# Attention and two expert layers on one core: four query chunks among the key chunks, another count of zeros, one reduction for the sums of squares

## The chip, the cores and the metric

The kernel runs on one core of one Trainium2 chip. The metric is the device time of one execution in microseconds (us); less is better. The engines are named as the profile names them: PE is TensorE's matmul, PEld its weight load, DVE is VectorE, ACT is ScalarE, POOL is GpSimd, and SP is SyncE, which issues every DMA of this kernel from one queue.

## What is computed

A kernel-feature attention feeds two layers one after the other. There are 4 x 576 = 2304 tokens, 8 heads of 64, 128 features, a model width of 512 and an inner width of 2048. All is float32.

```python
def phi(x):                                    # for queries and keys, scaled by D ** -0.25
    proj = np.einsum('bhsd,md->bhsm', x, omega)
    sq = np.sum(x * x, axis=-1, keepdims=True) / 2.0
    h = proj - sq
    h = h - np.max(h, axis=-1, keepdims=True)
    return np.exp(h) / np.sqrt(m)
kv = np.einsum('bhsm,bhsd->bhmd', k_p, v)
z = np.sum(k_p, axis=2)
num = np.einsum('bhsm,bhmd->bhsd', q_p, kv)
den = np.einsum('bhsm,bhm->bhs', q_p, z)[..., None] + 1e-06
x = num / den                                  # then tokens x 512
h = x @ w_in;  x = (h * np.cos(h)) @ w_out     # first layer
h = x @ w2_in; y = (h * np.clip(h + 3, 0, 6) / 6) @ w2_out   # second layer
```

## The kernel before

**Tiles and stages.** The tokens are cut into 18 chunks of 128. For each of 18 key chunks `chunk("k", c, ...)` loads a transposed tile `xT`, a plain tile `nat` and a value tile `v`; POOL squares `nat` and adds halves (L324, L328); DVE sums what is left per head into `sq` (`sums`, L334); PE projects `xT` with `omd` into two PSUM banks (L350); DVE takes the maximum per head (L363) and forms the bias (L370, L374); ACT takes the exponential of the two banks into two tiles `P` (L388, four instructions each); PE multiplies `P` with `v` into the running sums `kv` of a batch (L403). A query chunk goes the same way as far as `P`, is then transposed on PE (L433), copied by ACT into `qt`, multiplied with the finished `kvs` of its batch (L446), normalised on DVE (`rd`, `xn`: L456, L460, L467), transposed back (L481) and copied by ACT into `xx`. A query chunk needs the `kvs` of its batch only, and a batch is 4.5 chunks long.

The first layer's first half (8 of 16 inner tiles) of the first 1024 tokens runs as 16 "pair slots" (L711 into the bank `h`, L737 out to `kv`) between the query chunks. A slot's nonlinearity is two DVE steps (L651, L657), a sine on ACT (L661), a product on DVE (L664), a rounding on ACT and a difference on DVE. Exponentials and sines use different tables on ACT, so the sines of two slots stand behind the exponentials of two query chunks. After the last query chunk come "slots" of up to 512 tokens (L780 in, L802 out). All weights arrive as 64-bit numbers (`ws`, 512 KB a half tile) and are turned into two float32r parts by ACT and by five DVE steps (L559, L563, L569, L575, L261).

**What sets the order.** Nothing is scheduled on the chip. `Plan.order` plays the program through on the host: each task has a key (a due time in us), a modelled duration on its engine, and rings of buffers (`RINGS`); at each moment an engine takes the task with the smallest key that can start. The result is the order of instructions on each engine. A key chunk's key is `T_K * c`, a query chunk's `t_q + T_Q * p + 3 * (c % 2)` with `t_q = T_K * NCH`, so query chunks follow the key chunks. A key chunk's two banks come in turn from the rings `at`, `pt` and `h` of two banks each; a query chunk's from `at` alone.

**Zeros.** Where the plan has PE idle, the last loop puts matmuls of a zero tile (64 columns) on PE, whose results are not used: L872 while a `kv` sum is open, L875 while a pair slot's sum is open, L881 else. Their number is the planned idle time times `FILL_SHARE`, divided by `T_FILL`:

```python
for _ in range(int((now - idle) * FILL_SHARE / T_FILL) if f else 0):
```

One zero is one MATMUL of the program and two rows of the trace, since a float32 matmul runs in two passes.

Of the kernel before, what the change touches and what calls it, by code (L numbers as in the profile page):

```python
# [12 lines left out]
ALU = mybir.AluOpType  # L13
# [22 lines left out]
N_WARM = 5  # L36
N_PAIR = NCH // 2
N_A = 4
# [11 lines left out]
W_GATE = {}  # L50
PER = 2
FILL = 64
T_FILL = 0.115
FILL_SHARE = 0.8
LAT = {"t": 0.27, "a": 0.17, "v": 0.13, "p": 0.15, "d": 2.0}
# [142 lines left out]
def attention_moe_moe2_kernel(  # L198
# [95 lines left out]

    t_q = T_K * NCH

    def chunk(kind, c, k, exp_after, lead):
        u = (kind, c)
# [17 lines left out]

        pr = ("at", "pt", "h")[c % 3] if isk else "at"

        def square(e):
# [9 lines left out]

        def sums(e):  # L330

            sq = tile_of(ap, SQ, "sq", [128, 8])
            for hf in range(2):
                nc.vector.tensor_reduce(  # L334
                    out=sq[:, 4 * hf:4 * hf + 4], in_=buf[A].rearrange("p (h d) -> p h d", h=8)[:, hf:8:2, 0:32], axis=AX.X, op=ALU.add
                )

        add(("sqn",) + u, k - 3.5, {"p": 1.1}, square, use=[A])
        add(("sqh",) + u, k - 2, {"p": 0.7}, halve, [("sqn",) + u], use=[A])
        add(SQ, k - 0.5, {"v": 0.5}, sums, [("sqh",) + u], alloc="sq", use=[A])  # L340

        P0, P1 = ("pj", kind, c, 0), ("pj", kind, c, 1)
        before = [("pj", kind, c - 1, 1)] if c else [] if isk else [("pj", "k", NCH - 1, 1)]
        add(P0, k - 0.2, {"t": 0.01}, lambda e: bank(P0, pr), before, alloc=pr, use=[X])
# [23 lines left out]
        def bias1(e):  # L368
            mx = buf[MX]
            nc.vector.scalar_tensor_tensor(out=mx[:, 8:16], in0=buf[SQ], scalar=-0.5 * SCALE * SCALE, in1=mx[:, 0:8], op0=ALU.mult, op1=ALU.add)  # L370

        def bias2(e):
            mx = buf[MX]
            nc.vector.scalar_tensor_tensor(out=mx[:, 16:24], in0=buf[SQ], scalar=-0.5 * SCALE * SCALE, in1=mx[:, 8:16], op0=ALU.mult, op1=ALU.subtract)  # L374

# [3 lines left out]
        for hf in range(2):  # L379
            E = ("e", kind, c, hf)  # L380

            def exps(e, hf=hf, E=E):
                pj, mx = buf["pj", kind, c, hf], buf[MX]
                p = tile_of(ap, E, "P", [128, 512])
                for h in range(4):
                    o = slice(128 * h, 128 * h + 128)
                    b = 16 + 4 * hf + h
                    nc.scalar.activation(out=p[:, o], in_=pj[:, o], func=ACTF.Exp, bias=mx[:, b:b + 1])  # L388

            add(E, k + 1.5 + 0.1 * hf, {"a": 1.25 + (1.3 if exp_after and hf == 0 and c % PER == 0 else 0.0)}, exps,  # L390
                [("b2",) + u] + exp_after + ([("e", kind, c, 0)] if hf else []), alloc="P", use=[("pj", kind, c, hf), MX])
# [98 lines left out]

    for c in range(NCH):
        chunk("k", c, T_K * c, [], 6)
    n_a = N_A * NG // 2

    def period(g):

        return 1 + g // 2 if PER == 2 else min(3 + g, NCH - 1)

    for c in range(NCH):
        p = c // 2  # L500
        prior = [("sn", g) for g in range(n_a) if period(g) == c // PER - 1]
# [193 lines left out]
    def pair_slot(g):  # L695
# [259 lines left out]
```

## Time and profile before

| | us |
|---|---|
| median of 3 runs | 998.49 |
| lowest and highest | 998.3, 999.55 |
| the profiled execution, its own time | 997.92 |
| its span, first to last instruction | 996.1 |
| PE busy in the span | 985.5 |
| DVE, ACT, POOL busy | 599.0, 441.4, 90.6 |

A row of the timeline gives start and duration in us, the engine, the line, what it writes from what, shapes and count; behind it in brackets the idle time of the engine just before and what ended it. The ends of matmuls are modelled and overlap the next one's start, so a group's length is read from its start to the next one's start. A row of the stretches gives for each engine the busy time, the granted clock of PE as a share of full speed, and the busy share and rate of the DMA engines.

### The profile page before, as it was taken

How to read it: one execution, taken by the hardware profiler on the slowest of the kernel's cores; microseconds unless marked ns; L12 is line 12 of the kernel's file. 1: busy time of each engine (PE TensorE's matmuls, PEld its weight loads, DVE VectorE, ACT ScalarE, POOL GpSimd, SP SyncE). 2: the span in 40 equal slices, each digit the busy share in tenths (PEclk: the TensorE clock that was granted, in tenths of full speed). 3: DMA queues.
4: the chain of work that ended last, by engine and by line, in shares of the span. 5: the costliest groups of instructions: out<-in, count | busy, mean ns of one | idle time of the engine just before them, and what ended most of it. 6: DMA issues, size and time to landing. Idle time of an engine off the chain costs nothing.

```text
span 996.1 us, 16910 instructions
## 1 busy us (share of the span) xinstructions
PE 985.5 (99%) x6830; PEld 860.1 (86%) x6830; DVE 599.0 (60%) x1207; ACT 441.4 (44%) x888; POOL 90.6 (9%) x103
## 2 busy tenths in 40 slices
PE   9999999999999999999999999999999999999998
PEld 8899998989898889888888898888888888888898
DVE  5887788545569998999956599723223222322322
ACT  4775566555654545444332344424223322422332
POOL 5542134100000000010000000000000000000000
PEclk9999999999999999999999999999999999999999
DMA  8974344111012333332311014101000100100010
GB/s 278 331 246 151 107 136 140 33 44 33 2 42 86 110 101 107 106 117 81 118 55 43 1 50 132 64 1 43 1 1 1 42 1 1 43 1 1 1 43 22
DMA packets 32269, 72.59 MB, mean 73 GB/s; under 512 B 3392, under 2 KB 7488, under 8 KB 32192
## 3 DMA queue, kind: packets, MB, share of 16 engines
q1 hardware_dynamic: 32192, 71.52, 22.1%
q8 instruction: 53, 0.87, 0.4%
q14 instruction: 24, 0.20, 0.1%
HBM read 62.07 MB, written 9.44 MB: 72 GB/s over the span
## 4 chain that ended last, share of the span: by engine, by line
PE 97%; ACT 1%; DMA 1%; issue 0%; SPq 0%
PE at L780 18%; PE pt L780 18%; PE kv L802 18%; PE h L802 18%; PE h L711 5%; PE kv L737 5%; PE kv L881 3%; PE kv L872 3%; PE pt L446 2%; PE at L350 2%; PE kv L403 2%; PE kv L875 2%; PE pt L433 1%; PE pt L481 1%; DMA ws<-w 1%; PE pt L350 1%
## 5 line engine op out<-in xcount | busy, mean ns | idle before, releaser
L261 DVE TENSOR_TENSOR gl<-wk,gh 128x512 fp32r<-128x512 f32 (+1 forms) x160 | 104.3, 652 | 127.1 <-ACT gh L254 119.5
L254 ACT ACTIVATE gh<-wk 128x512 fp32r<-128x512 f32 (+1 forms) x160 | 94.4, 590 | 157.2 <-PE h L802 122.7
L780 PE MATMUL at<-mxh,wl 128*128 128x512 f32 (+1 forms) x288 | 105.3, 366 | 0.0
L780 PE MATMUL at<-mxh,wh 128*128 128x512 f32 (+1 forms) x288 | 105.3, 366 | 0.0
L802 PE MATMUL kv<-gh,wl 128*128 128x512 f32 (+1 forms) x288 | 105.3, 366 | 0.0
L802 PE MATMUL kv<-gh,wh 128*128 128x512 f32 (+1 forms) x288 | 105.3, 366 | 0.0
L780 PE MATMUL pt<-mxh,wl 128*128 128x512 f32 (+1 forms) x288 | 105.3, 366 | 0.0
L802 PE MATMUL h<-gh,wl 128*128 128x512 f32 (+1 forms) x288 | 105.3, 365 | 0.0
L780 PE MATMUL pt<-mxl,wh 128*128 128x512 f32 (+1 forms) x288 | 105.2, 365 | 0.0
L780 PE MATMUL at<-mxl,wh 128*128 128x512 f32 (+1 forms) x288 | 105.2, 365 | 0.0
L802 PE MATMUL kv<-gl,wh 128*128 128x512 f32 (+1 forms) x288 | 105.2, 365 | 0.0
L780 PE MATMUL pt<-mxh,wh 128*128 128x512 f32 (+1 forms) x288 | 105.2, 365 | 0.0
L802 PE MATMUL h<-gl,wh 128*128 128x512 f32 (+1 forms) x288 | 105.2, 365 | 0.0
L802 PE MATMUL h<-gh,wh 128*128 128x512 f32 (+1 forms) x288 | 105.2, 365 | 0.0
L661 ACT ACTIVATE wk<-wk,halfpi 128x512 f32<-128x512 f32 (+1 forms) x80 | 54.4, 681 | 91.5 <-DVE wk L657 91.3
L256 POOL TENSOR_SCALAR mxh<-xx 128x512 fp32r<-128x512 f32 (+1 forms) x25 | 20.3, 813 | 666.2 <-DVE mxl L261 258.0
L678 DVE SCALAR_TENSOR_TENSOR wk<-wk,at 128x512 f32<-128x512 f32 (+1 forms) x40 | 25.4, 635 | 70.3 <-ACT wk L672 70.2
L678 DVE SCALAR_TENSOR_TENSOR wk<-wk,pt 128x512 f32<-128x512 f32 (+1 forms) x40 | 25.4, 636 | 67.2 <-ACT wk L672 66.9
L780 PEld LDWEIGHTS pt<-mxh,wl 128*128 128x128 f32 x288 | 54.4, 189 | 8.9
L802 PEld LDWEIGHTS h<-gh,wh 128*128 128x128 f32 x288 | 54.4, 189 | 8.9
L780 PEld LDWEIGHTS pt<-mxh,wh 128*128 128x128 f32 x288 | 54.3, 189 | 8.9
L780 PEld LDWEIGHTS at<-mxl,wh 128*128 128x128 f32 x288 | 54.3, 189 | 8.9
(97 smaller groups left out, 2069.0 us busy)
## 6 DMA issues: line engine op xcount, KB each, us to landing
ws<-w SPq DMA_DIRECT2D x64, 512.0 KB, 3.7
v<-vn SPq DMA_DIRECT2D x18, 260.0 KB, 4.5
nat<-kn SPq DMA_DIRECT2D x18, 256.0 KB, 5.2
xT<-qT SPq DMA_DIRECT2D x18, 256.0 KB, 2.8
nat<-qn SPq DMA_DIRECT2D x18, 256.0 KB, 3.7
xT<-kT SPq DMA_DIRECT2D x17, 256.0 KB, 5.2
yy<-yp SPq DMA_DIRECT2D x16, 256.0 KB, 2.2
yp<-yy SPq DMA_DIRECT2D x16, 256.0 KB, 4.0
```

The costliest lines, as they stand in the source:

```text
L254: nc.scalar.activation(out=o, in_=i, func=ACTF.Copy)
L256: nc.gpsimd.tensor_scalar(out=o, in0=i, scalar1=1.0, scalar2=0.0, op0=ALU.mult, op1=ALU.add)
L261: (nc.gpsimd if e == "p" else nc.vector).tensor_tensor(out=o, in0=a, in1=b, op=ALU.subtract)
L350: nc.tensor.matmul(out=buf["pj", kind, c, o][:, 128 * i:128 * i + 128], lhsT=buf[X][64 * o:64 * o + 64, 128 * i:128 * i + 128], rhs=omd[64 ...
L661: nc.scalar.activation(out=r, in_=r, func=ACTF.Sin, scale=-TURN, bias=halfpi)
L678: nc.vector.scalar_tensor_tensor(out=w, in0=w, scalar=6.0, in1=hb(), op0=ALU.min, op1=ALU.mult)
L711: nc.tensor.matmul(out=o, lhsT=w[:, 128 * kc:128 * kc + 128], rhs=v, start=(kc == 0 and j == 0), stop=(kc == KC - 1 and j == 2), skip_grou ...
L737: nc.tensor.matmul(out=y, lhsT=w[:, o], rhs=v, start=(first and fi == 0 and j == 0 and ec % 2 == 0), stop=(last and fi == 1 and j == 2 and ...
L780: nc.tensor.matmul(out=buf["h", g][:, :n], lhsT=w[:, 128 * kc:128 * kc + 128], rhs=x, start=(kc == 0 and j == 0), stop=(kc == KC - 1 and j ...
L802: nc.tensor.matmul(out=buf["y", bi, ec][:, :n], lhsT=w[:, o], rhs=x, start=(first and j == 0), stop=(last and j == 2),)
L872: return lambda: nc.tensor.matmul(out=buf["kv", b, hf][:, 0:FILL], lhsT=zero[:, 0:128], rhs=zero[:, 0:FILL], start=False, stop=False, skip ...
L881: return lambda: nc.tensor.matmul(out=buf["fill", ring][:, 0:FILL], lhsT=zero[:, 0:128], rhs=zero[:, 0:FILL], start=True, stop=True)
```

## The change

There are three edits. (1) The first four query chunks (`N_EARLY`) stand in the planner's sequence at places 6, 8, 10 and 12 (`K_EARLY`), among the key chunks. `before` links of the projections follow that sequence. From place 6 on, the banks alternate between `at` and `h`, since `pt` is now used by the transposes; the first six key chunks still use three rings. `t_q` grows by four `T_K`, the query chunks after them and the pair slots get new due times (the first two slots' sines now stand behind the exponentials of query chunks 4 and 5, not 2 and 3). (2) The number of zeros is computed from 0.24 us for each, after 0.5 us of the gap are left out, rounded. (3) `sums` reduces all eight heads in one instruction; the bias steps read the sums through a reordered view.

```diff
-N_PAIR = NCH // 2
+N_EARLY = 4
+K_EARLY = 6
-PER = 2
-T_FILL = 0.115
-FILL_SHARE = 0.8
+T_FILL = 0.24
+FILL_SKIP = 0.5
...
-    t_q = T_K * NCH
+    t_q = T_K * (NCH + N_EARLY)
...
-        pr = ("at", "pt", "h")[c % 3] if isk else "at"
...
-            for hf in range(2):
-                nc.vector.tensor_reduce(
-                    out=sq[:, 4 * hf:4 * hf + 4], in_=buf[A].rearrange("p (h d) -> p h d", h=8)[:, hf:8:2, 0:32], axis=AX.X, op=ALU.add
-                )
+            nc.vector.tensor_reduce(out=sq, in_=buf[A].rearrange("p (h d) -> p h d", h=8)[:, :, 0:32], axis=AX.X, op=ALU.add)
...
-        add(SQ, k - 0.5, {"v": 0.5}, sums, [("sqh",) + u], alloc="sq", use=[A])
+        add(SQ, k - 0.5, {"v": 0.38}, sums, [("sqh",) + u], alloc="sq", use=[A])
...
-        before = [("pj", kind, c - 1, 1)] if c else [] if isk else [("pj", "k", NCH - 1, 1)]
+        before = [("pj",) + prev + (1,)] if prev else []
...
-    for c in range(NCH):
-        chunk("k", c, T_K * c, [], 6)
...
-        return 1 + g // 2 if PER == 2 else min(3 + g, NCH - 1)
-
-    for c in range(NCH):
-        p = c // 2
-        prior = [("sn", g) for g in range(n_a) if period(g) == c // PER - 1]
-        chunk("q", c, t_q + T_Q * p + 3 * (c % 2), prior, 10)
+        return N_EARLY // 2 + 1 + g // 2
+
+    order = [("k", c) for c in range(NCH)]
+    for c in range(N_EARLY):
+        order.insert(K_EARLY + 2 * c, ("q", c))
+    prev = None
+    for i, (kind, c) in enumerate(order):
+        pr = ("at", "pt", "h")[i % 3] if i < K_EARLY else ("at", "h")[i % 2]
+        chunk(kind, c, T_K * i, [], 6 if kind == "k" else 10, pr, prev)
+        prev = (kind, c)
+    for c in range(N_EARLY, NCH):
+        prior = [("sn", g) for g in range(n_a) if period(g) == c // 2]
+        chunk("q", c, t_q + T_Q * ((c - N_EARLY) // 2) + 3 * (c % 2), prior, 10, "at", prev)
+        prev = ("q", c)
...
-                slots.append((bi, 2 * fp, t_q + T_Q * (1 + s // 2) + 8 * (s % 2)))
+                slots.append((bi, 2 * fp, t_q + T_Q * (s / 2) + 4))
...
-        sn_after = [("e", "q", c, hf) for c in range(NCH) for hf in range(2) if c // PER == period(g)]
+        sn_after = [("e", "q", c, hf) for c in range(NCH) for hf in range(2) if c // 2 == period(g) - 1]
...
-                    for _ in range(int((now - idle) * FILL_SHARE / T_FILL) if f else 0):
+                    for _ in range(int((now - idle - FILL_SKIP) / T_FILL + 0.5) if f else 0):
```

The program of before has 294 zeros, that of after 66. Up to the first pair slot's matmul it has 208 and 44, behind that 86 and 22. Of real work PE has, up to that matmul, 168 projection matmuls, 320 value products, 28 transposes and 32 query products before, and 184, 304, 48 and 64 after; the work of all stages together is the same.

On PE, in the middle of the key chunks, before (L350 is a projection, L403 a product with values, L872 zeros; the numbers in names are buffers):

```order
L350 MATMUL at<-omd,xT 128x128 x8
L403 MATMUL kv_774<-v,P 64x65 x8
L872 MATMUL kv_774<-zero 128x64 x4
L350 MATMUL pt<-omd,xT 128x128 x8
L403 MATMUL kv_833<-v,P 64x65 x8
L403 MATMUL kv_774<-v,P 64x65 x8
L872 MATMUL kv_774<-zero 128x64 x4
L350 MATMUL h<-omd,xT 128x128 x8
L403 MATMUL kv_833<-v,P 64x65 x8
L872 MATMUL kv_774<-zero 128x64 x10
L403 MATMUL kv_774<-v,P 64x65 x8
L872 MATMUL kv_774<-zero 128x64 x8
```

and after, a little earlier in the key chunks (L351, L404 and L879 are the same three; L434, L447 and L482 are a query chunk's transposes, its product and its transpose back):

```order
L434 MATMUL pt<-ident,P 128x128 x4
L447 MATMUL pt<-kvs,qt 64x65 x8
L404 MATMUL kv_460<-v,P 64x65 x8
L447 MATMUL pt<-kvs,qt 64x65 x8
L351 MATMUL h<-omd,xT 128x128 x8
L404 MATMUL kv_493<-v,P 64x65 x8
L482 MATMUL pt<-ident,xn 128x128 x4
L434 MATMUL pt<-ident,P 128x128 x4
L879 MATMUL kv_460<-zero 128x64 x4
L351 MATMUL at<-omd,xT 128x128 x8
```

A query chunk's four kinds of PE work now stand between two key chunks, with few zeros or none, and the projections go to two rings in turn.

On PE, from the last key chunk's products to the first pair slot, before:

```order
L403 MATMUL kv_1169<-v,P 64x65 x8
L881 MATMUL kv_1381<-zero 128x64 x10
L433 MATMUL pt<-ident,P 128x128 x4
L881 MATMUL kv_1381<-zero 128x64 x6
L350 MATMUL at<-omd,xT 128x128 x8
L433 MATMUL pt<-ident,P 128x128 x4
L446 MATMUL pt<-kvs,qt 64x65 x8
L881 MATMUL kv_1381<-zero 128x64 x8
L446 MATMUL pt<-kvs,qt 64x65 x8
L881 MATMUL kv_1381<-zero 128x64 x17
L481 MATMUL pt<-ident,xn 128x128 x4
```

and after (L718 is L711 of before):

```order
L351 MATMUL at<-omd,xT 128x128 x8
L404 MATMUL kv_1439<-v,P 64x65 x8
L879 MATMUL kv_1382<-zero 128x64 x5
L718 MATMUL h<-mxh,wh_77 128x256
L718 MATMUL h<-mxh,wl_78 128x256
L718 MATMUL h<-mxl,wh_77 128x256
L718 MATMUL h<-mxh,wh_77 128x256
L718 MATMUL h<-mxh,wl_78 128x256
L718 MATMUL h<-mxl,wh_77 128x256
L404 MATMUL kv_1382<-v,P 64x65 x8
```

The stretch of query chunks with nothing but zeros between their steps is gone; the first pair slot starts before the last key chunk's products.

On DVE, in the key chunks, before (L363 the maxima, L334 the sums):

```order
L363 TENSOR_REDUCE mx<-pt 128x4
L575 SCALAR_TENSOR_TENSOR wt<-ws,wt 128x512
L370 SCALAR_TENSOR_TENSOR mx<-sq,mx 128x8
L334 TENSOR_REDUCE sq<-nat 128x4 x2
L374 SCALAR_TENSOR_TENSOR mx<-sq,mx 128x8
```

and after (L364 the maxima, L330 the sums, L457, L461 and L468 a query chunk's normalising):

```order
L364 TENSOR_REDUCE mx<-h 128x4
L582 SCALAR_TENSOR_TENSOR wt<-ws,wt 128x512
L371 SCALAR_TENSOR_TENSOR mx<-sq,mx 128x8
L330 TENSOR_REDUCE sq<-nat 128x8
L375 SCALAR_TENSOR_TENSOR mx<-sq,mx 128x8
L364 TENSOR_REDUCE mx<-at 128x4
L261 TENSOR_TENSOR wl_80<-wt,wh_79 128x512
L457 TENSOR_SCALAR rd<-pt 128x4
```

One reduction stands where there were two, and a query chunk's steps stand among those of the key chunks. Ahead of the first pair slot's L651 (L658 after), DVE has 44 maxima, 44 sums, 42 bias steps, 53 steps on `wt`, 13 on `wl` and 12 normalising steps before, and 46, 24, 46, 49, 10 and 24 after. Ahead of the first sine, ACT has 176 exponentials, 6 `qt`, 2 `xx`, 13 `wh` and 16 `wt` before, and 192, 11, 5, 12 and 15 after. SP issues, ahead of the last value tile, 9 halves of weights and 6 query tiles before, 12 and 13 after.

## Rows read from the trace of the kernel before

**Rows 1.** The page's first part: busy time of each engine, its share of the span, instructions.

```profile
PE 985.5 (99%) x6830; PEld 860.1 (86%) x6830; DVE 599.0 (60%) x1207; ACT 441.4 (44%) x888; POOL 90.6 (9%) x103
```

**Rows 2.** Who waited for whom, PE, 0 to 300 us: us in total, times, longest.

```profile
PE pt L446 <- ACT qt L254: 3.3, 3, 1.1
```

**Rows 3.** Groups of instructions by line, PE, the zeros: count, busy us, mean ns, idle before.

```profile
L872 PE MATMUL kv<-zero 128*128 128x64 f32 x216 | 28.6, 280 | 0.0
L881 PE MATMUL kv<-zero 128*128 128x64 f32 x228 | 27.8, 275 | 0.5 <-ACT kvs L254 0.5
L875 PE MATMUL kv<-zero 128*128 128x64 f32 x144 | 17.2, 275 | 0.0
```

**Rows 4.** Timeline of PE: three runs of zeros and what follows each.

```profile
44.75 2.44 PE L872 MATMUL kv<-zero 128*128 128x64 f32 x20
47.13 1.16 PE L350 MATMUL at<-omd,xT 64*128 64x128 f32 x16
...
93.56 4.01 PE L881 MATMUL kv<-zero 128*128 128x64 f32 x34
97.41 0.61 PE L481 MATMUL pt<-ident,xn 128*128 128x128 f32 x4
...
102.72 3.79 PE L881 MATMUL kv<-zero 128*128 128x64 f32 x32
106.34 0.61 PE L481 MATMUL pt<-ident,xn 128*128 128x128 f32 x4
```

**Rows 5.** Timelines of ACT and DVE: the work that the matmuls behind those zeros need (the exponentials that free the bank `at`, and the normalised tiles).

```profile
44.69 1.14 ACT L388 ACTIVATE P<-at,mx 128x128 f32<-128x128 f32 x4
...
94.75 0.42 DVE L467 TENSOR_TENSOR xn<-pt,rd 128x256 f32<-128x256 f32 x1
...
103.98 0.41 DVE L467 TENSOR_TENSOR xn<-pt,rd 128x256 f32<-128x256 f32 x1
```

**Rows 6.** Timelines of DVE, ACT and PE: the first maximum, the first exponentials, the first matmul of a pair slot, its first DVE step, the first sine, the first matmul of a slot.

```profile
6.50 0.69 DVE L363 TENSOR_REDUCE mx<-at 128x4 f32<-128x512 f32 x1 [3.70 <-PE at L350]
10.33 1.28 ACT L388 ACT_TABLE_LOAD   x1 [10.33 <-DVE mx L374]
110.89 0.37 PE L711 MATMUL h<-mxh,wh 128*128 128x256 f32 x1
115.50 0.69 DVE L651 TENSOR_SCALAR wk<-h 128x512 f32<-128x512 f32 x1 [0.47 <-PE h L711]
121.85 0.72 ACT L661 ACTIVATE wk<-wk,halfpi 128x512 f32<-128x512 f32 x1
290.49 0.40 PE L780 MATMUL at<-mxh,wh 128*128 128x512 f32 x1
```

**Rows 7.** The chain that ended last, 84 to 125 us: start, us that count on the chain, what.

```profile
88.79 1.09 PE at L350 x16
93.02 0.62 PE pt L446 x16
97.57 0.44 PE pt L481 x4
...
113.11 2.35 PE h L711 x18
```

**Rows 8.** Busy time in stretches: PE, PEld, DVE, ACT and POOL (with counts), granted clock, DMA share, GB/s.

```profile
30.00:40.00 10.00, 8.58 (x138) 7.57 (x138) 8.10 (x21) 6.89 (x23) 3.48 (x4) 1.00 0.99 342
0.00:115.50 115.50, 111.88 (x1538) 102.88 (x1539) 87.39 (x213) 69.60 (x213) 50.89 (x59) 1.00 0.70 232
0.00:121.80 121.80, 118.18 (x1611) 108.73 (x1612) 92.30 (x227) 74.19 (x224) 50.89 (x59) 1.00 0.68 223
10.00:84.00 74.00, 72.39 (x1154) 66.32 (x1150) 61.30 (x152) 53.69 (x174) 40.81 (x42) 1.00 0.84 280
84.00:111.00 27.00, 26.51 (x291) 25.26 (x286) 19.58 (x48) 13.67 (x36) 6.21 (x8) 1.00 0.37 119
121.80:290.60 168.80, 165.53 (x1766) 154.86 (x1765) 106.76 (x271) 104.56 (x224) 26.10 (x27) 1.00 0.20 61
300.00:500.00 200.00, 200.00 (x973) 169.42 (x973) 184.83 (x343) 95.71 (x162) 7.86 (x10) 1.00 0.32 103
```

**Rows 9.** Timeline of DVE in the key chunks: two sums, a bias step, a maximum, a step on `wt`.

```profile
62.63 0.46 DVE L334 TENSOR_REDUCE sq<-nat 128x4 f32<-128x128 f32 x2
63.01 0.15 DVE L370 SCALAR_TENSOR_TENSOR mx<-sq,mx 128x8 f32<-128x8 f32 x1
...
64.68 0.68 DVE L363 TENSOR_REDUCE mx<-at 128x4 f32<-128x512 f32 x1
65.28 0.68 DVE L569 SCALAR_TENSOR_TENSOR wt<-ws,wt 128x512 uint32<-128x512 uint32 x1
```

**Rows 10.** Timelines of PE and ACT: the seventh key chunk's projection; the exponentials of the key chunk that was projected into `at` at 47.13, and the next projection into `at`.

```profile
22.97 1.16 PE L350 MATMUL at<-omd,xT 64*128 64x128 f32 x16
...
54.31 1.15 ACT L388 ACTIVATE P<-at,mx 128x128 f32<-128x128 f32 x4 [1.85 <-DVE mx L374]
59.02 0.66 ACT L555 ACTIVATE wt<-ws 128x512 f32<-128x512 f32 x1 [3.56 <-DMA ws<-w]
59.58 1.14 ACT L388 ACTIVATE P<-at,mx 128x128 f32<-128x128 f32 x4
...
60.69 1.24 PE L350 MATMUL at<-omd,xT 64*128 64x128 f32 x16
```

More of the change, by code (lines that the diff above doesn't have):

```diff
@@ L293, in attention_moe_moe2_kernel, with chunk @@
     kv_parts = {(b, hf): [] for b in range(B) for hf in range(2)}
-    t_q = T_K * NCH
-    def chunk(kind, c, k, exp_after, lead):
+    t_q = T_K * (NCH + N_EARLY)
+    def chunk(kind, c, k, exp_after, lead, pr, prev):
         u = (kind, c)
@@ L332, in sums, with sq_of, four @@
             sq = tile_of(ap, SQ, "sq", [128, 8])
-            for hf in range(2):
-                nc.vector.tensor_reduce(
-                    out=sq[:, 4 * hf:4 * hf + 4], in_=buf[A].rearrange("p (h d) -> p h d", h=8)[:, hf:8:2, 0:32], axis=AX.X, op=ALU.add
-                )
+            nc.vector.tensor_reduce(out=sq, in_=buf[A].rearrange("p (h d) -> p h d", h=8)[:, :, 0:32], axis=AX.X, op=ALU.add)
+        def sq_of():
+            return buf[SQ].rearrange("p (i o) -> p o i", o=2)
+        def four(a):
+            return a.rearrange("p (o i) -> p o i", o=2)
         add(("sqn",) + u, k - 3.5, {"p": 1.1}, square, use=[A])
         add(("sqh",) + u, k - 2, {"p": 0.7}, halve, [("sqn",) + u], use=[A])
-        add(SQ, k - 0.5, {"v": 0.5}, sums, [("sqh",) + u], alloc="sq", use=[A])
+        add(SQ, k - 0.5, {"v": 0.38}, sums, [("sqh",) + u], alloc="sq", use=[A])
         P0, P1 = ("pj", kind, c, 0), ("pj", kind, c, 1)
-        before = [("pj", kind, c - 1, 1)] if c else [] if isk else [("pj", "k", NCH - 1, 1)]
+        before = [("pj",) + prev + (1,)] if prev else []
         add(P0, k - 0.2, {"t": 0.01}, lambda e: bank(P0, pr), before, alloc=pr, use=[X])
@@ L369, in bias1 @@
             mx = buf[MX]
-            nc.vector.scalar_tensor_tensor(out=mx[:, 8:16], in0=buf[SQ], scalar=-0.5 * SCALE * SCALE, in1=mx[:, 0:8], op0=ALU.mult, op1=ALU.add)
+            nc.vector.scalar_tensor_tensor(out=four(mx[:, 8:16]), in0=sq_of(), scalar=-0.5 * SCALE * SCALE, in1=four(mx[:, 0:8]), op0=ALU.mult, op1=ALU.add)
         def bias2(e):
             mx = buf[MX]
-            nc.vector.scalar_tensor_tensor(out=mx[:, 16:24], in0=buf[SQ], scalar=-0.5 * SCALE * SCALE, in1=mx[:, 8:16], op0=ALU.mult, op1=ALU.subtract)
+            nc.vector.scalar_tensor_tensor(out=four(mx[:, 16:24]), in0=sq_of(), scalar=-0.5 * SCALE * SCALE, in1=four(mx[:, 8:16]), op0=ALU.mult, op1=ALU.subtract)
         add(("b1",) + u, k + 1.2, {"v": 0.2}, bias1, [("mx", kind, c, 1)], use=[MX, SQ])
@@ L388, in exps @@
                     nc.scalar.activation(out=p[:, o], in_=pj[:, o], func=ACTF.Exp, bias=mx[:, b:b + 1])
-            add(E, k + 1.5 + 0.1 * hf, {"a": 1.25 + (1.3 if exp_after and hf == 0 and c % PER == 0 else 0.0)}, exps,
+            add(E, k + 1.5 + 0.1 * hf, {"a": 1.25 + (1.3 if exp_after and hf == 0 and c % 2 == 0 else 0.0)}, exps,
                 [("b2",) + u] + exp_after + ([("e", kind, c, 0)] if hf else []), alloc="P", use=[("pj", kind, c, hf), MX])
@@ L489, in chunk @@
         add(("xx", c), k + 7.5, {"a": 0.62}, put, use=[("xt", c)])
-    for c in range(NCH):
-        chunk("k", c, T_K * c, [], 6)
     n_a = N_A * NG // 2
     def period(g):
-        return 1 + g // 2 if PER == 2 else min(3 + g, NCH - 1)
-    for c in range(NCH):
-        p = c // 2
-        prior = [("sn", g) for g in range(n_a) if period(g) == c // PER - 1]
-        chunk("q", c, t_q + T_Q * p + 3 * (c % 2), prior, 10)
+        return N_EARLY // 2 + 1 + g // 2
[11 more added lines that the diff above has]
+        prev = ("q", c)
     all_exp = [("e", "q", c, hf) for c in range(NCH) for hf in range(2)]
     all_att = [("xx", c) for c in range(NCH)]
-    t_m = t_q + T_Q * N_PAIR
+    t_m = t_q + T_Q * (NCH - N_EARLY) / 2 + 8
     blocks = [dict(m=1, t0=256 * b, n=256, fs=range(0, NG), mode="pair") for b in range(N_A)]
-    blocks += [dict(m=1, t0=t0, n=n, fs=range(0, NG), mode="part") for t0, n in ((1024, 512), (1536, 512), (2048, 256))]
+    blocks += [dict(m=1, t0=t0, n=n, fs=range(0, NG), mode="part") for t0, n in [(t0, min(512, NT - t0)) for t0 in range(256 * N_A, NT, 512)]]
     n_g1 = len(blocks)
```

## The prediction

> **What bounds the kernel now.** I read the busy times first: PE works for 985.5 of 996.1 us, every other engine at most 60% [rows 1]. Then the waits: PE's longest kind in the first 300 us comes to 3.3 us in total [rows 2]. So the time is PE's list of instructions, and what matters is what is in it. The groups by line show 216 + 228 + 144 = 588 rows of zeros [rows 3], 294 instructions, all before the first slot of 512 columns at 290.49 [rows 6]. Behind that point nothing is changed, and PE is 100% busy at least to 500 us [rows 8]. So I looked at how long a zero takes, and at whether the thing that it waits for is late or early.
>
> A zero's length is read from start to start. The three runs take 2.38, 3.85 and 3.62 us for 10, 17 and 16 zeros, together 9.85 us for 43, or 0.229 us each [rows 4]. (Two rows a zero, so about 0.115 us a row: the planner of before counted one of the two.) And the zeros run past what they wait for. The exponentials that free the bank `at` end at 45.83, the projection into it starts at 47.13. The normalised tiles end at 95.17 and 104.39, their transposes start at 97.41 and 106.34 [rows 4, 5]. That is 1.3, 2.2 and 2.0 us late: 5.5 of 9.85 us, or 56%, was surplus, and the rest covers a real wait.
>
> **The zeros.** 294 become 66: 228 x 0.23 = **52.4 us** of PE's list go, 164 x 0.23 = 37.7 ahead of the first pair slot, 64 x 0.23 = 14.7 behind it. This is the most that the change can give on PE. Not all of it stays: where a zero covered a wait, the wait comes back as idle time.
>
> The page "TensorE: Matmul & The Clock Gate" of the Trainium skill, section "Back-to-back issue gap", gives a warm matmul its columns over 2.4 GHz plus 2.5 ns; for 64 columns that is an estimate of 29 ns a row, and the removed zeros would be worth 13 us. Its section "LDWEIGHTS" gives a load 128 columns over 1.2 GHz, 107 ns by estimate, and with that the removed zeros are worth 49 us. The runs of zeros decide for the second: a row takes 115 ns [rows 4].
>
> **The early query chunks.** They move work ahead of the first pair slot. The instruction counts there change by +16 projections, -16 value products, +20 transposes and +32 query products. By the chain's rows these cost 1.09 / 8, 0.62 / 8 (a value product has the same 65 columns), 0.44 / 4 and 0.62 / 8 us [rows 7]: 2.2 - 1.2 + 2.2 + 2.5 = +5.7 us ahead, and 5.7 less behind. What is bought: between 84 and 111 us PE did nearly nothing but 80 zeros and the steps of two or three query chunks, each of which waits for the one before on another engine; DVE was busy for 19.58 and ACT for 13.67 of 27 us [rows 8]. These steps now stand between key chunks.
>
> PE alone would reach the first pair slot at 110.9 - 37.7 + 5.7 = 78.9 us. **DVE cannot follow.** Up to the slot's first DVE step at 115.50 it was busy for 87.39 us [rows 6, 8]. The counts ahead of that step change by +2 maxima (0.60 each, start to start), 44 sums to 24 wider ones, +4 bias steps (0.15 at most), -4 `wt` and -3 `wl` steps (0.6 each, one 0.35) and +12 normalising steps (0.42, 0.15 and 0.15 at most) [rows 5, 9]. The wider sum isn't in the trace. Two narrow ones take 0.38 [rows 9]; it reads the same 256 elements, so it costs no more than 0.38 and no less than half a maximum of 512, 0.30. I take 0.33, nearer the lower row because one instruction's start is saved: 24 x 0.33 = 7.9 against 22 x 0.38 = 8.4. Sum: 1.2 - 0.5 + 0.6 - 2.1 - 1.8 + 2.9 = +0.3. DVE's work up to the slot is the same, 87 us, and the third edit is worth half a us here, 1.8 us over 36 chunks, nearly all of it beside other work.
>
> DVE's work starts at 6.5, with 0.5 us done before. Never idle, it would reach the slot's first step at 6.5 + 86.9 = 93.4; as busy as between 10 and 84 us, 61.30 of 74.00 or 83% [rows 8], at 6.5 + 86.9 / 0.83 = 111. In the trace it was PE that DVE waited for; now PE waits for DVE, so I take a value near the full end, 95%: **98.0 us instead of 115.5, -17.5 us.** Of the 37.7 us of zeros about half comes back as PE waiting for exponentials.
>
> ACT is second. Up to the first sine it was busy for 74.19 us [rows 8]. It gets 16 exponentials more (1.15 / 4 each at most), 5 `qt` and 3 `xx` (0.6 like the 0.66 step [rows 10]) and loses two weight steps: 4.6 + 4.8 - 1.3 = +8 us. From 10.33 on that ends at 92.5 if it never waits, so the first sine is not before that; DVE's path gives 98 + some 5 us for the last exponentials, so ACT hides behind DVE as long as its waits for weight halves (3.56 us in one [rows 10]) sum to under 10 us.
>
> On SP's one queue three more weight halves and seven more query tiles stand ahead of the last value tile: 3 x 0.52 + 7 x 0.26 = 3.4 MB (a half is 128 rows of 512 64-bit numbers, a tile of 128 x 512 float32 half of that), 10 us at the 342 GB/s of a full stretch [rows 8]. Before, the stretch 10:84 moved 280 GB/s at a share of 0.84, so 16% of 74 us, 12 us, was free. It fits, with little over; what is queued behind a late tile is every later tile. I cost it at nothing, at worst at those 10 us, within the 83% end above.
>
> **Behind the slot.** The list from there to 290.49 loses 14.7 us of zeros and the 5.7 us of query work; before, PE was idle for 168.80 - 165.53 = 3.3 us of it [rows 8]. The share of real waits under zeros, 44% of 14.7, is 6.5 us at most; the gaps now keep at least half a microsecond without zeros, so I take +4 us of new waits, bounds 0 and 10. In the stretch 300 to 500, DVE is busy for 184.83 of 200 us [rows 8]; its work and PE's there are the same, so both move together and nothing is lost.
>
> **Sum.** -17.5 - 14.7 - 5.7 + 4 = **-33.9 us**. The span of 996.1 becomes 962.2; the execution's own time is 1.8 us above its span, so 964.0. The profiled execution, 997.92, is 0.6 under the median of the runs, too little to correct for. A check from the other side: if the zeros lose just their surplus, 0.56 x 52.4 = 29 us go, which gives 969 without any gain from hiding the query chunks.
>
> **Rivals.**
>
> *Nearer the floor.* DVE at 100% and no new waits: -22.1 - 20.4 = -42.5, 955; a few us less if DVE's steps, some of which are stretched in the key chunks, shorten. For it: DVE has more ready work at hand. I give less than 952 a chance of 0.08.
>
> *The banks set the pace; this one ends slower.* From place 6 on, two sets of banks serve the projections, where there were three. The set `at` was projected into at 47.13 and again at 60.69, a turn of 13.6 us [rows 4, 10]. With two sets and that turn a chunk takes 6.8 us; the projection at place 6 starts near 23 us, as the seventh did [rows 10], the one at place 22, just ahead of the first pair slot, 16 x 6.8 = 109 us later at 132, 21 us after 110.9. With -14.7 - 5.7 + 4 behind it the kernel ends 5 us slower, at about 1003. It decides from a turn of 13 us: at 13 the pair slot starts at 127 and the time is that of before. For it: the trace has such turns. Against: 3.56 of the 13.6 us were ACT standing behind a weight load, and DVE placed other work first because there was a third set; the steps alone are 1.09 + 1.2 + 0.3 + 2 x 1.15 us and a few hops, some 6 us, and the early slots use the planner's own ring count. A turn of 9 us gives 23 + 72 = 95 at place 22, which is in the forecast; turns of 10 to 12.5 give 103 to 123 and times of 977 to 996. Chances: 0.04 for slower, 0.09 for that middle.
>
> *The zeros covered waits.* Then all 52 us come back as idle time, and the time stays at 998. Against it stand the three late starts [rows 4, 5]. 0.03.
>
> *The clock.* It was granted in full (1.00, 2.4 GHz) in each stretch, also between 30 and 40 us, where PE was busy for just 8.58 of 10 [rows 8]; the zeros may be why. At the lower level, 1.2 GHz, each us of PE work costs another: 34 us of PE's work done there eat the whole gain. Chance 0.04, half of it slower. The same page, Part 1, has the array throttled by default and put back to half rate when it goes idle; no stretch of this trace shows that.
>
> **How the numbers follow.** Forecast (955 to 977): 0.72. Below 952: 0.08. Banks in the middle: 0.09. Banks, slower: 0.04. Clock: 0.04. Zeros no surplus: 0.03. About 0.2%, 2 us, is what a measurement of this kernel can tell from no change. Faster: 0.72 + 0.08 + 0.09 + 0.02 = 0.91; same 0.03; slower 0.06. The range takes in DVE's two ends (955, and 111 us at the slot: -4.5 - 20.4 + 4 = 977) and a few us for the new waits: 950 to 981; some 0.2 is outside.
>
> **What would show it.** 132 rows of zeros instead of 588, 0.23 us a pair. PE's waits, 6 us now, near 25 us and mostly ahead of 100 us, for `P` from ACT. The first DVE step of a pair slot at 98 (93 to 111), DVE busy for 87 us up to it. The first slot of 512 columns near 250 us, since 8 us of pair work (66 matmuls of 0.12 to 0.13 us, 2.35 / 18 [rows 7]) now stand behind its start. A clock of 1.00 throughout. The forecast is wrong if the projections wait for banks (PE idle at the projections, with DVE idle as well), if PE waits for loads, if the granted clock falls, or if behind the first pair slot PE waits for over 10 us.

## The result, and the profile after

The median is **966.64 us** (4 runs, 965.72 to 968.68) beside 998.39 for the kernel before on the same chip (997.77 to 999.55): a ratio of 0.9683, 95% interval 0.9664 to 0.9703. The profiled execution has a span of 964.1 us, where 962.2 was forecast; before it was 996.1.

The page's busy line of the kernel after; it answers to [rows 1]:

```profile
PE 949.9 (99%) x6374; PEld 822.2 (85%) x6374; DVE 600.9 (62%) x1174; ACT 436.2 (45%) x885; POOL 91.5 (9%) x101
```

The groups by line, PE, of the kernel after: the zeros, 132 rows where there were 588 [rows 3].

```profile
L879 PE MATMUL kv<-zero 128*128 128x64 f32 x72 | 11.6, 294 | 0.0
...
L888 PE MATMUL kv<-zero 128*128 128x64 f32 x30 | 4.1, 278 | 0.0
L882 PE MATMUL kv<-zero 128*128 128x64 f32 x30 | 4.0, 280 | 0.0
```

Timelines of PE, DVE and ACT after: the four milestones of [rows 6] (first matmul of a pair slot, its first DVE step, the first sine, the first matmul of a slot).

```profile
101.58 0.36 PE L718 MATMUL h<-mxh,wh 128*128 128x256 f32 x1 [0.37 <-issue]
...
106.46 0.69 DVE L658 TENSOR_SCALAR wk<-h 128x512 f32<-128x512 f32 x1 [0.96 <-PE h L718]
...
117.29 0.72 ACT L668 ACTIVATE wk<-wk,halfpi 128x512 f32<-128x512 f32 x1
...
250.44 0.40 PE L787 MATMUL at<-mxh,wh 128*128 128x512 f32 x1
```

I divide the span at the first DVE step of a pair slot. It came at 106.46 us instead of 115.50: 9.0 us gained, where 17.5 were forecast. From there to the end it is 857.6 instead of 880.6 us: 23.0 gained, where 16.4 were forecast. **The total is right by luck: two errors of 8.5 and 6.6 us cancel.** (The slot at 250.44 is no such mark, since 8 us of pair work now stand behind it.)

Busy time in stretches after, columns as in [rows 8] (PE, PEld, DVE, ACT, POOL, granted clock, DMA share, GB/s):

```profile
0.00:106.46 106.46, 98.20 (x1308) 84.49 (x1309) 90.89 (x203) 72.09 (x228) 59.05 (x64) 0.89 0.77 252
...
70.00:83.50 13.50, 12.40 (x176) 10.85 (x176) 13.15 (x33) 10.07 (x33) 3.30 (x5) 1.00 0.82 260
83.50:97.20 13.70, 13.70 (x158) 12.08 (x156) 10.79 (x21) 8.08 (x27) 10.77 (x10) 0.50 0.61 208
106.50:250.00 143.50, 141.27 (x1543) 132.67 (x1542) 101.81 (x251) 100.17 (x216) 19.68 (x21) 1.00 0.23 73
```

PE idled for 106.46 - 98.20 = 8.3 us up to that step, not for some 25. But the clock, forecast at 1.00, was granted at 0.89 on the mean, and between 83.5 and 97.2 us at 0.50, its lower level of 1.2 GHz: PE is busy without a gap there because each step takes double (the rows below). Behind the step PE idled for 2.2 us in 143.5; the clock is 1.00.

The timeline of PE after, 16 rows of projections ahead of that stretch and 16 in it:

```profile
77.56 1.20 PE L351 MATMUL at<-omd,xT 64*128 64x128 f32 x16
...
87.53 2.47 PE L351 MATMUL at<-omd,xT 64*128 64x128 f32 x16
```

The chain that ended last, after, from 67 to 98 us (start, us that count on the chain, what):

```profile
67.44 0.60 DVE wt L576
68.04 0.60 DVE mx L364
68.64 0.86 DVE wt L582
...
69.55 3.64 DMA ws<-w
...
73.27 0.69 ACT wt L562
73.96 0.11 ACT P L389
...
74.73 4.70 DMA ws<-w
...
79.52 0.28 ACT wt L562
79.80 0.32 issue
80.12 1.14 ACT P L389 x4
81.26 0.52 ACT wh L254
81.78 1.04 ACT P L389 x4
...
82.86 1.49 PE h L351 x14
84.36 2.62 PE kv L404 x48
86.98 0.62 PE kv L879 x2
87.60 2.40 PE at L351 x16
```

So the chain isn't one engine. DVE ends a weight conversion; that frees the buffer for the next half of weights; the half lands 3.6 to 4.7 us later; ACT stands at its step on it with the exponentials behind; they free the bank; PE projects, at half clock, up to the pair slot.

The waits of PE after, 0 to 106.46 us (us in total, times, longest); [rows 2] was the longest kind before:

```profile
PE kv L404 <- ACT P L389: 2.5, 2, 1.3
PE h L351 <- ACT P L389: 1.4, 3, 0.9
...
PE pt L351 <- DMA xT<-kT: 1.1, 1, 1.1
PE at L351 <- ACT P L389: 1.1, 1, 1.1
```

And DVE had more work than the forecast's 87 us: 90.89. The groups by line of DVE, 0 to 115.5 us before and 0 to 106.46 after: the two bias steps (count, busy us, mean ns, idle before).

```profile
L374 DVE SCALAR_TENSOR_TENSOR mx<-sq,mx 128x8 f32<-128x8 f32 x21 | 6.6, 316 | 0.1
L370 DVE SCALAR_TENSOR_TENSOR mx<-sq,mx 128x8 f32<-128x8 f32 x21 | 5.8, 277 | 0.1
```

```profile
L375 DVE SCALAR_TENSOR_TENSOR mx<-sq,mx 128x8 f32<-128x8 f32 x23 | 10.0, 436 | 0.0
L371 DVE SCALAR_TENSOR_TENSOR mx<-sq,mx 128x8 f32<-128x8 f32 x23 | 9.0, 389 | 0.1
```

A step on eight numbers per partition took 296 ns on the mean before and 413 after: 12.4 us became 19.0. The forecast had added +0.6 us for four more of them, at 0.15 us from the one row in [rows 9].

### The profile page after: what moved, and what is told of

Same layout as the page of the kernel before. It is cut to its first block, busy times and chain, and to the rows that moved or that the text cites. A ratio compares the mean times of both kernels' runs of the same rounds, so it can differ in the third digit from the quotient of the medians.

```text
span 964.1 us, 15966 instructions
## 1 busy us (share of the span) xinstructions
PE 949.9 (99%) x6374; PEld 822.2 (85%) x6374; DVE 600.9 (62%) x1174; ACT 436.2 (45%) x885; POOL 91.5 (9%) x101
## 4 chain that ended last, share of the span: by engine, by line
PE 89%; DVE 5%; DMA 2%; ACT 1%; POOL 0%; issue 0%; SPq 0%; ACTq 0%; POOLq 0%; DVEq 0%
PE at L787 18%; PE pt L787 18%; PE kv L809 18%; PE h L809 18%; PE kv L744 5%; PE h L718 5%; PE at L351 2%; DVE mx L364 2%; PE pt L447 1%; PE kv L404 1%; DMA ws<-w 1%; PE pt L434 1%; DMA nat<-qn 1%; DVE wt L582 1%; DVE mx L375 1%; PE pt L482 1%
## 5 line engine op out<-in xcount | busy, mean ns | idle before, releaser
L256 POOL TENSOR_SCALAR mxh<-xx 128x512 fp32r<-128x512 f32 (+1 forms) x23 | 18.0, 785 | 654.4 <-DVE mxl L261 257.3
L809 PEld LDWEIGHTS h<-gh,wl 128*128 128x128 f32 x288 | 54.3, 189 | 8.9
```

Source lines behind the costliest of these rows:

```text
L256: nc.gpsimd.tensor_scalar(out=o, in0=i, scalar1=1.0, scalar2=0.0, op0=ALU.mult, op1=ALU.add)
L809: nc.tensor.matmul(out=buf["y", bi, ec][:, :n], lhsT=w[:, o], rhs=x, start=(first and j == 0), stop=(last and j == 2),)
```

## The experiments

Every kernel below, by its median and its ratio to the kernel before; "u1" is the first DVE step of a pair slot, "rest" the span from there to the end; granted clock and DVE's busy time are those up to u1; "zeros" are those ahead of the first pair slot. The first two columns are of 3 to 12 runs, the others of the one profiled run, whose own time can differ from the median by up to 3 us (cancel: 940.02). The kernel before, run beside them, had medians of 998.25 to 998.78.

| | us | ratio, 95% interval | u1 | rest | clock | DVE busy | zeros |
|---|---|---|---|---|---|---|---|
| before | 998.4 | | 115.5 | 880.6 | 1.00 | 87.4 | 208 |
| after | 966.6 | 0.966 to 0.970 | 106.5 | 857.6 | 0.89 | 90.9 | 44 |
| zeros_only | 982.7 | 0.980 to 0.987 | 105.7 | 874.1 | 0.89 | 93.0 | 72 |
| order_old_zeros | 977.4 | 0.974 to 0.983 | 110.8 | 864.7 | 1.00 | 94.7 | 154 |
| skip0 | 971.6 | 0.968 to 0.979 | 108.3 | 859.0 | 0.97 | 94.6 | 102 |
| no_zeros | 968.5 | 0.966 to 0.974 | 109.3 | 857.4 | 0.84 | 95.2 | 0 |
| sums_only | 997.1 | 0.996 to 1.001 | 115.2 | 879.9 | 1.00 | 91.3 | 201 |
| less_dve | 963.5 | 0.961 to 0.966 | 101.7 | 857.1 | 0.93 | 76.6 | 44 |
| no_pool | 958.7 | 0.957 to 0.963 | 99.4 | 857.2 | 0.93 | 76.9 | 44 |
| double_pool | 980.1 | 0.978 to 0.983 | 118.4 | 859.1 | 0.84 | 104.1 | 44 |
| less_both | 957.9 | 0.953 to 0.965 | 100.3 | 856.8 | 0.93 | 65.2 | 44 |
| no_pool_skip0 | 962.7 | 0.957 to 0.966 | 103.1 | 859.5 | 0.95 | 77.1 | 102 |
| no_plain | 953.2 | 0.950 to 0.960 | 93.3 | 858.1 | 0.99 | 76.2 | 44 |
| cancel | 943.3 | 0.938 to 0.946 | 85.3 | 852.9 | 1.00 | 70.0 | 30 |

### Which part of the change, and how many zeros

**zeros_only**: the kernel before with the second edit alone.

```diff
-T_FILL = 0.115
-FILL_SHARE = 0.8
+T_FILL = 0.24
+FILL_SKIP = 0.5
```

> The order of before with the new rule for the zeros alone: 109 zeros instead of 294. By my prediction's reckoning 185 x 0.23 = 42.5 us leave PE's list and the surplus share, 56%, is gained: about 24 us, so 972 to 978. If the zeros covered real waits: 996 to 1000. If the granted clock falls in the new gaps and that costs much: 982 to 992, with stretches of 0.5 in the clock.

982.72: 15.7 us are gained, half of the whole change. The clock falls to its lower level for 23.9 us in three stretches ahead of 90 us, and PE's waits come back in small pieces (5.1 us for `qt`). The reading with clock and real waits holds; the forecast's "check from the other side", 29 us from the zeros' surplus alone, doesn't. Beside it, after's u1 is no earlier (106.5 and 105.7), though it has the early query chunks done by then; what the new order adds shows behind u1, 857.6 instead of 874.1.

**order_old_zeros**: after's order and sums, the old count of zeros.

```diff
-for _ in range(int((now - idle - FILL_SKIP) / T_FILL + 0.5) if f else 0):
+for _ in range(int((now - idle) * 0.8 / 0.115) if f else 0):
```

> The changed order and the wider sum with the old rule for the zeros: 215 zeros, 154 of them ahead of the first pair slot. If DVE sets the pace of the key chunks (my theory), most of the 25 us of additional zeros ahead of the slot fall into PE's waits and only the 9 us behind it count in full: 975 to 982, granted clock 1.00. If the clock's fall in the changed kernel is what holds it back, its return offsets a good part: 966 to 972.

977.39, with the clock at 1.00, in the range of the theory. The order and the sums alone thus bring 21.0 us and the zeros alone 15.7; both together bring 31.8, so the two overlap by 5. Here 110 more zeros stand ahead of u1, worth 25 us of PE, and u1 comes only 4.3 us later than after. Waiting time that they fill is the smaller part: PE's idle time up to u1 falls from 8.3 to 3.5 us. The larger part is work that PE no longer does at half clock, some 12 us by an estimate (half of after's 23.9 us at the lower level). Behind u1 39 more zeros, 9.0 us, cost 864.7 - 857.6 = 7.1: these cost nearly in full.

**skip0** and **no_zeros**: after with more zeros (`FILL_SKIP = 0`) and with none (`range(0)`).

> The changed kernel with the half microsecond no longer left out of a gap: 142 zeros, 102 of them ahead of the first pair slot. If DVE sets the pace, the clock returns to full but the first pair slot comes within 3 us of where it was (101.6) and the zeros behind cost 2 to 4 us: 965 to 970. If the 24 us at the lower clock hold the key chunks back, the slot comes some 7 us earlier: 959 to 963.

> The changed kernel with no zero at all behind the first five. If DVE sets the pace, the clock is low for longer but the time moves little: 962 to 972. If the clock sets the pace: 976 to 1000, with the granted clock low for 50 us or more.

971.62, 1.6 us above the range (its four runs spread from 969.1 to 978.4, at mean clocks of 0.986 to 0.996), and 968.48, within it. From 102 zeros to none, u1 stays within 106.5 and 109.3, while the clock goes from 0.97 to 0.84. So neither the zeros nor the clock alone places u1 in after's order. Behind u1, the last 22 zeros cost nothing: without them the rest is 857.4, the same. skip0's 18 more, 4.1 us, cost 1.4.

**sums_only**: the kernel before with the third edit alone.

> The kernel before with the third edit alone (one reduction of eight heads, 36 of them in place of 72 narrow ones, and the bias steps through the reordered view); 280 zeros. Forecast's price: 0.33 us for a wide sum against 0.38 for two narrow ones, nearly all beside PE's work: 996.5 to 999, within 0.2% of before. Rival, the reordered view makes the bias steps dearer: DVE's work up to the first DVE step of a pair slot grows instead of falling by 1 us; and a third, the 14 zeros fewer alone bring 3 us: 995 to 996.

997.11, not to be told from no change, as forecast. A wide sum took 0.33 to 0.34 us from start to start, as forecast. But DVE's work up to u1 grew from 87.4 to 91.3, 3.0 of it in its bias steps (12.4 to 15.4): the mark that was set for a dearer view. The trace says that the view isn't it. Where no POOL instruction stands beside them, these steps take 0.15 us in sums_only (22 of 44) and 0.16 before, with the plain view (23 of 42); the others take 0.54 and 0.46. And zeros_only, with the plain view, has a mean of 348 ns beside sums_only's 349.

### What stretches DVE's steps

The timelines of DVE and POOL after, 86 to 93 us:

```profile
86.49 0.69 DVE L371 SCALAR_TENSOR_TENSOR mx<-sq,mx 128x8 f32<-128x8 f32 x1
...
87.70 0.68 DVE L375 SCALAR_TENSOR_TENSOR mx<-sq,mx 128x8 f32<-128x8 f32 x1
...
92.05 0.68 DVE L371 SCALAR_TENSOR_TENSOR mx<-sq,mx 128x8 f32<-128x8 f32 x1
```

```profile
85.98 2.38 POOL L326 TENSOR_TENSOR nat<-nat 128x256 f32<-128x256 f32 x2
...
90.31 2.39 POOL L326 TENSOR_TENSOR nat<-nat 128x256 f32<-128x256 f32 x2
```

The three steps end at 87.18, 88.38 and 92.73. POOL's first pair of 1.19 us each ends at 87.17 and 88.36, the second pair at 92.70: each small DVE step ends as an instruction of POOL ends. So it is with 22 of after's 23 bias steps of over 0.3 us, within 0.05 us. The page "SBUF — State Buffer" of the Trainium skill, section "SBUF: two separate sides", has a pair of ports that VectorE and GpSimd share, which one of them holds for a whole instruction while the other waits; these rows agree.

**no_pool**: after, with `square` and `halve` returning at once. **double_pool**: a second square per chunk, into a spare tile.

```diff
+nc.gpsimd.tensor_tensor(out=spare, in0=a, in1=a, op=ALU.mult)
```

> POOL's squares and halvings are left out (DVE sums the plain tile in their place), DVE's own list is as in after. Theory, DVE's bias steps and weight steps are stretched while POOL works: the bias steps fall from a mean of 0.33 to 0.38 us to 0.1 to 0.2, DVE's work up to the first DVE step of a pair slot from 91.4 to 80 to 86 us, that step to 93 to 101 us and the time to 952 to 961. Rival, they are long for another reason (they wait on their inputs): their mean stays above 0.3 and the time at 963 to 968.

> POOL does each chunk's square a second time into a spare tile that nobody reads; all else as in after. Theory, POOL's work stretches DVE's steps: DVE's work up to the first DVE step of a pair slot grows by 3 to 8 us, that step comes at 109 to 116, the time is 969 to 978. Rival, no such effect (or POOL's own lateness alone counts): that work stays within 1.5 us of 91.4 and the time at 964 to 968, unless the sums themselves wait for POOL, which the waits of DVE on POOL would show.

The groups of bias steps, 0 to u1, in no_pool and in double_pool:

```profile
L373 DVE SCALAR_TENSOR_TENSOR mx<-sq,mx 128x8 f32<-128x8 f32 x23 | 4.1, 180 | 0.1
L377 DVE SCALAR_TENSOR_TENSOR mx<-sq,mx 128x8 f32<-128x8 f32 x23 | 3.8, 166 | 0.0
```

```profile
L377 DVE SCALAR_TENSOR_TENSOR mx<-sq,mx 128x8 f32<-128x8 f32 x23 | 13.9, 606 | 0.0
L373 DVE SCALAR_TENSOR_TENSOR mx<-sq,mx 128x8 f32<-128x8 f32 x23 | 10.8, 470 | 0.1
```

With the same reordered view the step means 173 ns without POOL, 413 with it and 538 with more of it. DVE's work up to u1 goes 76.9, 90.9, 104.1: shown. It moved by 14 us down and 13 up, more than either expectation; 11.1 of the 14 are bias steps, most of the others weight steps. double_pool, at 980.12, is slower than its range; no_pool, at 958.69, is within. u1 follows by 12 us upwards, by 7 downwards. (In double_pool the sums also wait longer for POOL, 5.0 us instead of 2.4, so not all of the 12 need be the stretching.)

### What comes next when DVE has less to do

**less_dve**: after, without 25 of DVE's steps on `wt`.

> Some 25 of the five-step conversions' DVE steps on wt (the clamps and signs of the first eight inner tiles of the first layer) are left out, about 13 us of DVE work ahead of the first pair slot; order of all else, zeros and POOL work as in after. Theory, DVE's work paces the key chunks: the first DVE step of a pair slot comes at 93 to 97 us instead of 106.5, the time at 953 to 958. Rival, PE (zeros, granted clock, hand-overs) paces them: that step stays at 104 to 107 and the time at 964 to 968.

963.51, between the two ranges. 14.3 us of DVE's work are gone and u1 gains 4.8: the theory that DVE alone paces the key chunks falls. DVE's time without work ahead of u1 grows from 15.6 to 25.0 us.

**less_both**: no_pool and less_dve together. **no_pool_skip0**: no_pool with `FILL_SKIP = 0`.

> POOL's squares and halvings and the 25 clamps and signs on wt are both left out; all else, zeros too, as in after. Each alone took 14 us of DVE's work ahead of the first pair slot's DVE step (90.9 to 77) and brought that step 7.0 and 4.8 us forward. Theory, DVE is the only pace: that work falls to 62 to 66 us, the step comes at 86 to 93, the time is 944 to 952. Rival, with DVE at 77 us PE at the lower granted clock and its hand-overs with ACT are the pace already: the step stays at 96 to 100, DVE idles for over 25 us ahead of it, the time is 954 to 959.

> POOL's squares and halvings are left out and no part of a gap is left without zeros: 142 zeros, 102 ahead of the first pair slot, where there were 66 and 44. Theory, the stretches at the lower granted clock (13.7 us ahead of the slot without POOL's work) cost time now that DVE has room: the zeros keep the clock at 1.00 for all but 4 us, the first DVE step of a pair slot comes at 93 to 97 us, the time is 951 to 956. Rival, the zeros cost PE what the clock gives back: that step at 98 to 104, the time at 957 to 964.

957.89 and 962.65: the rivals. With 11.7 us less DVE work than no_pool, u1 doesn't move (100.3 beside 99.4). In no_pool_skip0's profiled run 58 zeros more didn't keep the clock: it is low from 83.3 to 93.6, and u1 is 3.7 us later. Two of its four runs did keep a mean clock of 1.00 and took 960.7, beside 964.5 and 965.3 of the others; that is within no_pool's own 956.4 to 961.1 at 0.991 to 0.994. So here the zeros cost what the clock gives back, if not more. The chain of less_both, 73 to 89 us, says what is late:

```profile
73.63 0.34 DVE sq L332
73.97 0.03 issue
74.00 6.44 DMA ws<-w
...
80.52 0.66 ACT wt L564
81.18 1.04 ACT P L391 x4
...
82.27 2.07 PE at L353 x14
84.34 2.12 PE kv L406 x32
...
88.77 2.01 PE h L353 x16
```

A half of weights takes 6.44 us to land, ACT stands at its step on it with the exponentials behind, PE waits 2.9 us for its bank, and then works at half clock. While the half was on its way the DMA engines were busy for 0.98 of the time, at 329 GB/s, near the 342 of a full stretch.

**no_plain**: no_pool without the plain tiles' loads on the one queue; DVE's sums read the transposed tile instead, so its list and the order stay.

```diff
-lambda e: nc.sync.dma_start(out=tile_of(ap, A, "nat", [128, 512]), in_=(kn if isk else qn)[c]), alloc="nat")
+lambda e: None, alloc="nat")
...
-nc.vector.tensor_reduce(out=sq, in_=buf[A].rearrange("p (h d) -> p h d", h=8)[:, :, 0:32], axis=AX.X, op=ALU.add)
+nc.vector.tensor_reduce(out=sq, in_=buf[X].rearrange("p (h d) -> p h d", h=8)[:, :, 0:32], axis=AX.X, op=ALU.add)
```

> POOL's squares and halvings are left out as before, and the 36 loads of plain tiles (9.4 MB) on the one queue too; DVE's reductions read the transposed tile, so DVE's list and the order on every engine stay. Without POOL the chain went, from 73.27 us, over a weight half that took 6.36 us to land, ACT's step on it, the exponentials queued behind that, and PE at the lower granted clock from 80.7 to 91.0. Theory, the late halves are the second pace and bring on the low clock: ACT's waits for halves in the first 100 us fall from 9.8 to under 6 us, the clock stays at 1.00 but for 4 us or less, the first DVE step of a pair slot comes at 88 to 94 instead of 99.4, the time is 946 to 953. Rival, the planned order of PE and ACT with 77 us of DVE work sets it, whatever the queue does: the step at 97 to 101, the clock low near 80 to 91 again, the time 956 to 961.

953.15; u1 at 93.3, 6.2 us earlier than in no_pool at the same DVE work, the clock at 1.00 up to 91.4. The rival is out. ACT's waits for halves fell to 6.9 us from 9.8, less than expected: the one of 3.58 us that ends at 79.72 in no_pool is 1.05 us here and ends at 74.38. But a later one of 3.24 us, ending at 88.76, stands on the chain in its place:

```profile
82.67 6.01 DMA ws<-w
...
88.76 0.66 ACT wt L564
...
89.73 1.11 PE kv L406 x16
90.84 2.40 PE h L720 x12
```

So in the profiled runs the loads were the second pace, and late halves still stand ahead of u1. (By all runs the gain is less certain: 949.5 to 959.2 us beside no_pool's 956.4 to 961.1.) How much of the 6.2 us is the order of the one queue, how much the bytes on full DMA engines and how much the clock, this run doesn't separate. That late halves bring on the low clock holds for the profiled run and not for all: of the four runs one took 949.5 at a mean clock of 1.00, two 953.0 and 953.3 at 0.998, and one 959.2 at 0.987.

**cancel**: a version that beats both. The sum of squares of a token is the same for all its features, so it drops out of `h - max(h)`; the program need not compute it.

```diff
-        add(("sqn",) + u, k - 3.5, {"p": 1.1}, square, use=[A])
-        add(("sqh",) + u, k - 2, {"p": 0.7}, halve, [("sqn",) + u], use=[A])
-        add(SQ, k - 0.5, {"v": 0.38}, sums, [("sqh",) + u], alloc="sq", use=[A])
...
+            nc.vector.tensor_scalar(out=mx[:, 16:24], in0=mx[:, 0:8], scalar1=-1.0, scalar2=None, op0=ALU.mult)
```

> After with the sums of squares left out of the program, since they cancel against the maximum that is taken behind them: no plain tiles are loaded (36 tiles less), POOL has no squares or halvings, DVE no sums and one bias step for two; the planner orders the rest anew and places 36 zeros, 30 ahead of the first pair slot. Theory, DVE's work and POOL's beside it pace the key chunks: DVE's work ahead of the first DVE step of a pair slot falls to 64 to 70 us, the step comes at 86 to 95, the time is 944 to 953. Rival, PE at the lower clock and its hand-overs with ACT take the place of DVE: the step at 96 to 101, DVE idle for over 25 us ahead of it, the granted clock low for over 25 us, the time 954 to 960.

**943.25**, ratio 0.9422 (0.9383 to 0.9460), just under the range. The profiled run is its fastest, 940.02: u1 at 85.3, the clock at 1.00; the others have mean clocks of 0.992 to 0.996. The stretch up to u1 of cancel:

```profile
0.00:85.28 85.28, 80.73 (x1280) 70.42 (x1281) 70.03 (x161) 71.03 (x229) 3.30 (x10) 1.00 0.72 229
```

PE, DVE and ACT are all near full now: DVE 70.0 and ACT 71.0 of 85.3 us, of which the first 6 and 9 are a start.

## Why the prediction came out as it did

The time was forecast within 2 us, but by two errors that cancel. Of the signs that the forecast named for its being wrong, one came: the granted clock fell. The others came in small size: 2.5 us of waits for banks at the projections, 1.1 us for a load, 2.2 us behind u1.

- **What bounds the kernel: right.** PE's list set the time; 36 us of busy time went with 32 us of span.
- **The zeros: right in size, with a cost that was missed.** The surplus was there: behind u1, order_old_zeros' 39 more cost nearly their length (7.1 of 9.0 us), and after's own 22 nothing. But with the zeros away the clock falls ahead of u1: in zeros_only three stretches, in after four, together 23.9 us. The forecast gave the falling clock 0.04 and expected 1.00. The page "TensorE: Matmul & The Clock Gate" of the Trainium skill, Part 1, which has the array put back to half rate when it goes idle, agrees in direction: up to u1, PE idled for 3.6 us before at 1.00, for 8.3 after at 0.89, for 18.0 in no_zeros at 0.84. The idle time alone doesn't set it: 3.3 us went with 0.95 in no_pool_skip0, 4.6 with 1.00 in cancel. The forecast said that no stretch of the trace before shows such a fall; its last 3.1 us do, with PE idle and a clock of 0.77 on the mean. In after, a long idle stretch was not what came ahead of the fall: the longest wait in the 13.5 us before 83.5 was 0.9 us. And what came back of the zeros ahead of u1 was less PE waiting (4.6 us more than before), as forecast, than work at half clock (some 12 us, the estimate above).
- **"DVE cannot follow": right as the first pace, mis-sized.** In after and its variants with other zeros u1 follows DVE's work, 13.7 to 16.1 us behind it. The forecast had 86.9 us of work at 95%: 98.0. Measured were 90.9, of which 0.5 ahead of the first maximum at 6.6, at 90.4 / 99.85 = 91%: 106.5. Of the 8.5 us, the work is 3.8 (at 95% it would give 101.8) and the lower share 4.7. **The term of the sum that failed is that of the bias steps**: +0.6 us, from one short row of 0.15, where +6.6 were measured. The price hid that 42 of them already came to 0.30 on the mean; and that all of them would grow to 0.41, 5.4 of the 6.6 us, was put at nothing. POOL stretches them: up to u1 it was busy for 59.05 us in after instead of 50.89, and 26 of 46 bias steps stand beside one of its instructions instead of 19 of 42. That the early query chunks' squares are the reason is likely and not shown apart: zeros_only, in the old order, has 348 ns.
- **The 95%: too high.** DVE's own loop with the weight halves and PE at half clock stand between its steps; less_both shows that they hold u1 near 100 when DVE has 12 us less to do than in no_pool. The clock's own part in after looks small: one of its four runs had a mean clock of 0.996 instead of 0.988 or 0.989 and took 965.72, beside 965.89 to 968.68.
- **"SP's queue costs nothing, at worst 10 us": not nothing.** Without the plain tiles, u1 gains 6.2 us in no_plain. That run leaves out all plain tiles, not the three halves and seven query tiles of the term, and POOL's work too, so the term's size isn't shown.
- **Behind the slot: +4 us of new waits, measured -1.** PE idles for 2.2 us there, beside 3.3 before. That is 5 of the 6.6 us; the other 1.6 stay open. The gaps that kept no zeros were no waits: even without any zero the rest is 857.4.
- **ACT behind DVE: the first sine came 10.8 us after u1, not 5**, and no cost of it shows behind u1.
- **The banks' rival: out.** The projection at place 6 started at 23.07 and that at place 22 at 98.24, a turn of 9.4 us; 95 was given for a turn of 9. (The rival's middle times of 977 to 996 come to 974 to 994 by its own terms; nothing else hangs on them.)
- **The wide sum: right**, 0.33 to 0.34 from start to start beside 0.33, and of no account for the time.

## What to carry to other kernels

Price a short instruction by the mean of its group and not by a row that looks clean: where it shares something with another engine, the mean moves when the order moves. Before an engine is called the bound, take work away from it alone: here 14 us less on DVE brought 5, because late loads of weights and the hand-overs behind them came next. Look at the arithmetic as well: the largest gain, 23 us beyond the change, came from a sum that cancels.

## What the runs showed of the hardware

- A bias step on VectorE, 128x8 with both inputs in SBUF, took 0.15 to 0.16 us where no GpSimd instruction stood beside it, with the plain view and the reordered one. Beside GpSimd it lasted up to 1.00 us and ended as a GpSimd instruction ended. Reductions from PSUM (0.68 us) and the wide sums from SBUF (0.41 us) were the same with POOL's work and without.
- The granted clock fell to half for 13.7 us behind a stretch in which PE was busy for 12.40 of 13.50 us. 58 zeros more ahead of u1 didn't prevent such a stretch in two of the four runs of no_pool_skip0. With fewer loads the profiled run of no_plain had 1.9 us of it up to u1, but one of its four runs had a mean clock of 0.987.
